# Attention and two MLP layers on one core: x1 in DRAM in the order of the head pairs, read back in pieces of 64 rows

## The chip, the cores and the metric

One core of a Trainium2 chip runs the whole program in one launch. The metric is the device time of that launch in microseconds. Three runs of the kernel before took 959.88, 960.28 and 961.83 us; the median is 960.28 us.

## What is computed

Causal block attention for 4 batches of 8 heads (576 positions, head size 64, blocks of 64 positions), then two MLP layers without normalisation between them. The attention's output x1 has 512 features (8 heads of 64) for each of 2304 tokens.

```python
scores = scale * np.matmul(q, k.transpose(0, 1, 3, 2))   # (4, 8, 576, 576), block-causal mask
attn = softmax(scores)                                    # rows divided by sum + 1e-9
x = np.matmul(attn, v)                                    # (4, 8, 576, 64)
x1 = x.transpose(0, 2, 1, 3).reshape(2304, 512)
h = x1 @ w_in1                                            # 512 -> 2048
g = np.where(h >= 1, h, np.where(h <= -1, 0, (h + 1) ** 2 / 4))
x2 = g @ w_out1                                           # 2048 -> 512
h = x2 @ w_in2
out = (h * np.cos(h)) @ w_out2
```

## The kernel before, in words

The heads are worked on two at a time. A pair fills the 128 partitions with 2 heads of 64 features; 16 pairs cover 4 batches of 8 heads. The list `pairs` names them. The first four pairs (batch 0) are neighbouring heads: (0,1), (2,3), (4,5), (6,7). All later pairs are heads two apart: (0,2), (1,3), (4,6), (5,7), so that one load can bring K or Q of two pairs.

For each pair TensorE makes the scores (L589, the last 64 query rows in L655), ScalarE the exponentials (L605, L668), GpSimd the division (L635), TensorE transposes the probabilities (L692), and then multiplies with V: `pv` (L727) for the main part, `pv_halves` (L738) for what is left of it, `pv_tails` (L784) for the last 64 positions of two pairs. `pv` of pair n reads the tile `rv` (`M.V[n % 2]`, two buffers), which `load_v` fills with three kinds of DMA: L487 (main rows; `pv` waits for these), L491 (the last rows) and L494 (the rows for `pv_halves`). One period of the schedule (the table `PERIOD`) handles two pairs. In it the tails of a pair of pairs are the last readers of both V buffers, so the L487 loads of the next even pair go out only behind them; eight units of TensorE's work later in the table (scores and transposes) stands that pair's `pv`.

The result of a pair is copied out of PSUM to `xs` (128 partitions, 576 columns; three buffers) and stored to `x1d[b]`, a DRAM tile of 512 rows (8 heads of 64 features) and 576 columns: columns 0 to 511 in `pv_halves` (L768), the last 64 columns in `tail_halves` (L806). `x1_rows` (L404) gives the DRAM side of the store. `x1_keys` names what the store writes, for the planner.

Layer 1 works on blocks of two times 256 tokens (one block has a single 256). `x_load` (L820 on) brings a block's x1 back: for each of four groups of 128 features (`kk`) one DMA for each batch that the block touches, of 128 rows (L837). The first block takes x1 straight from `xs`. Then the weights of layer 1 are loaded (L263, L268), put together (ScalarE L280 and L289, VectorE L295), split in two parts, and used by `mm1` (L865) and `mm2` (L906). Weights of layer 2 are combined and written to DRAM between (L341). Layer 2 follows (L1048, L1140).

A planner (`Plan`) sets the order of the program on every engine: each operation has a cost, keys that it reads and writes, and the list of TensorE's own order is kept. All DMAs are issued by SyncE (SP), one after another in the planner's order; an instruction that waits there holds up the ones behind it. In particular SP issues, in this order, in each period: stores of x1, the V loads, then K and Q loads (L527) for later pairs.

```python
pairs = [(b, 2 * p, 2 * p + 1) for b in range(B) for p in range(NP)]
for n in range(NK, N):                       # NK = 4
    b, h, _ = pairs[n]
    pairs[n] = b, h // 4 * 4 + n % 2, h // 4 * 4 + n % 2 + 2
```

Of the kernel before, what the change touches and what calls it, by code (L numbers as in the profile page):

```python
# [9 lines left out]
F32 = mybir.dt.float32  # L10
# [92 lines left out]
def attn_moe_moe_kernel(ctx: ExitStack, tc: tile.TileContext, q, k, v, w_in1, w_out1, w_in2, w_out2, out):  # L103
    nc = tc.nc
    B, H, S, D = q.shape
# [6 lines left out]
    NP = H // 2  # L112
    N = B * NP
# [49 lines left out]
    x1d = [dram.tile([DM, S], F32, name=f"x1d{b}") for b in range(B)]  # L163
# [34 lines left out]
    def do(eng, cost, reads, writes, fn, lock="G", latency=0.0):  # L198
        plan.add(eng, cost, reads, writes, fn, lock, latency)

    def cp(engines, n, out, in_, reads, writes, scale=1.0):
        do(engines, costs(n, engines), reads, writes, lambda e: pin(copy(e, out(), in_(), scale)))

    def diff(engines, n, lo, raw, hi, reads, writes):
        c = {"V": 0.065 + n / 960.0, "G": 0.15 + 0.0022 * n}
        do(engines, {e: c[e] for e in engines}, reads, writes,
           lambda e: pin(rest(lo(), raw(), hi(), nc.gpsimd if e == "G" else nc.vector)), lock="GV")

    def dma(kb, reads, writes, fn):
        do("S", 0.1 + kb / 230.0, reads, writes, lambda e: fn(), latency=2.0)  # L210

    def issue(count, kb, reads, writes, fn, rate=230.0):
        do("S", 0.53 * count, reads, writes, lambda e: fn(), latency=2.0 + max(0.0, kb / rate - 0.53 * count))
# [27 lines left out]
    def x_view(half, kk):  # L241
        arena, off = x_home(half, kk)
        return (M.A1 if half else M.X).view(off, [2, 512], F32R)

    def x_keys(half, kk, part=None):
        arena, off = x_home(half, kk)
        return span(arena, off, 4 * KB) if part is None else span(arena, off + 2 * KB * part, 2 * KB)
# [124 lines left out]
    def split(i):  # L372
        return i > 1

    def pb(at_, b):
        n, i = at_
        if split(i):
            if b not in tiles[n]:
                tiles[n][b] = M.ps[1].tile([128, 512], F32, name=f"t{i}{b}", tag=f"t{i}{b}")
            return tiles[n][b]  # L380
        return whole(at_)[:, b]

    def whole(at_):
        n, i = at_
        if 0 not in tiles[n]:
            tiles[n][0] = M.ps[0].tile([128, 2, 512], F32, name=f"t{i}", tag=f"t{i}")
        return tiles[n][0]

    def bk(at_, b):
        return ("ps", at_[1], b if split(at_[1]) else 0)  # L390

    def bks(at_):
        return [("ps", at_[1], b) for b in range(2 if split(at_[1]) else 1)]

    pairs = [(b, 2 * p, 2 * p + 1) for b in range(B) for p in range(NP)]
    for n in range(NK, N):
        b, h, _ = pairs[n]
        pairs[n] = b, h // 4 * 4 + n % 2, h // 4 * 4 + n % 2 + 2

    def heads(n):  # L400
        _, h0, h1 = pairs[n]
        return slice(h0, h1 + 1, h1 - h0)

    def x1_rows(n, c0, c1):  # L404
        return x1d[pairs[n][0]].rearrange("(h d) s -> h d s", d=D)[heads(n), :, c0:c1]

    def x1_keys(n, part):
        b, h0, h1 = pairs[n]
        return [("x1d", b, h, part) for h in (h0, h1)]


    def tensor(cost, reads, writes, fn):
        do("P", cost + M.switch, reads, writes, lambda e: fn())
# [43 lines left out]
    def pt_view(u):  # L457
        return M.A2.view(PT_HOME[u], [128 * len(PT_BLOCKS[u])])

    def pt_of(i, j):  # L460
        u = i if i == "a" and j != "b" else "b" if i in ("a", "b") else LEFT if (i, j) == (4, 6) else 0 if i < 4 else 2 if i < 6 else 3
        return u, PT_BLOCKS[u].index((i, j))
# [272 lines left out]
    def quarters(at_, jobs):  # L735
        for rows, V, slot, PT, a, b, out_ in jobs:
            for h in range(2):
                pin(nc.tensor.matmul(  # L738
                    out=pb(at_, b)[64 * h:64 * h + 64, out_], lhsT=V[rows, slot, h, :],
                    rhs=PT[rows, a + 64 * (h if rows.start == 0 else 1 - h):][:, 0:64],  # L740
                    start=False, stop=True, skip_group_check=True,
                ))
# [3 lines left out]
    def pv_halves(n):  # L746
        at_ = half_open.pop(n)

        def emit():
            jobs = []  # L750
            for x in range(0, 4, 2):
                u, c = pt_of(2 * x, 2 * x + 2)
                for y, rows, slot in ((x, LOW, x), (x + 1, HIGH, LAST + 1 + x // 2)):
                    o = 128 * (y // 2)
                    jobs.append((rows, M.V[n % 2], slot, pt_view(u), 128 * c, y % 2, slice(o, o + 64)))
            quarters(at_, jobs)

        tensor(0.22, [("V", n % 2)] + [("PT", u, b) for u in (3, 2, 0) for b in range(2)], bks(at_), emit)
        xs = M.xs[n % 3]
        XS = [("xs", n % 3, b) for b in range(2)]  # L760
        to = lambda: xs[:, 0:512].rearrange("p (i b c) -> p b i c", b=2, c=128)
        if split(at_[1]):
            for x in range(2):
                cp("AV", 256, lambda x=x: to()[:, x], lambda x=x: pb(at_, x)[:, 0:256].rearrange("p (i c) -> p i c", c=128),
                   [bk(at_, x)], [XS[x]])
        else:
            cp("AV", 512, to, lambda: whole(at_)[:, :, 0:256].rearrange("p b (i c) -> p b i c", c=128), [bk(at_, 0)], XS)
        issue(1, 256, XS, x1_keys(n, 0), lambda: nc.sync.dma_start(out=x1_rows(n, 0, 512), in_=xs[:, 0:512]))  # L768
        if n < NK:
            t = lambda: x_view(1, n)  # L770
            cp("AG", 512, lambda: t()[:, 0], lambda: xs[:, 0:512], XS, x_keys(1, n, 0))
            diff("V", 512, lambda: t()[:, 1], lambda: xs[:, 0:512], lambda: t()[:, 0],
                 XS + x_keys(1, n, 0), x_keys(1, n, 1))
# [17 lines left out]
    def tail_halves(n):  # L791
        at_ = half_open.pop(("t", n))

        def emit():
            u, c = pt_of("a", "b")
            quarters(at_, [
                (rows, M.V[(n + x) % 2], LAST, pt_view(u), 128 * c, x, slice(0, 64))
                for x, rows in ((0, LOW), (1, HIGH))
            ])

        tensor(0.11, [("V", c) for c in range(2)] + [("PT", u, b) for u in "ab" for b in range(2)], bks(at_), emit)
        for x in range(2):
            m = n + x
            xs = M.xs[m % 3]
            cp("AV", 64, lambda xs=xs: xs[:, 512:S], lambda x=x: pb(at_, x)[:, 0:64], [bk(at_, x)], [("xt", m % 3)])
            issue(1, 32, [("xt", m % 3)], x1_keys(m, 1), lambda xs=xs, m=m: nc.sync.dma_start(  # L806
                out=x1_rows(m, 512, S), in_=xs[:, 512:S]
            ))

# [12 lines left out]
    def x_load(kb):  # L822
        x_half, js = 1 - kb % 2, blocks[kb]
        w = NB * len(js)
        for kk in range(NK):
            t = lambda kk=kk: x_view(x_half, kk)
            pieces, need, done = [], [], 0
            while done < w:
                b, c = divmod(js[0] * NB + done, S)
                n = min(w - done, S - c)  # L830
                need += [("x1d", b, 2 * kk + h, part) for h in range(2) for part in range(2) if (c < 512, c + n > 512)[part]]
                pieces.append((b, c, n, done))
                done += n

            def emit(t=t, kk=kk, pieces=pieces):
                for b, c, n, done in pieces:
                    nc.sync.dma_start(  # L837
                        out=t()[:, 1, done:done + n].bitcast(F32), in_=x1d[b][128 * kk:128 * (kk + 1), c:c + n]
                    )

            dma(w // 2, need, x_keys(x_half, kk, 1), emit)
            cp("AG", w, lambda t=t: t()[:, 0, 0:w], lambda t=t: t()[:, 1, 0:w].bitcast(F32),
               x_keys(x_half, kk, 1), x_keys(x_half, kk, 0))
            diff("V", w, lambda t=t: t()[:, 1, 0:w], lambda t=t: t()[:, 1, 0:w].bitcast(F32),
                 lambda t=t: t()[:, 0, 0:w], x_keys(x_half, kk, 0), x_keys(x_half, kk, 1))
# [452 lines left out]
    def part_one():  # L1298
# [15 lines left out]
        for n in range(2):  # L1314
# [5 lines left out]
        units = {  # L1320
            "tl": tails, "pk": lambda n, t=0: prepare(n, 0, t), "pq": lambda n, t=0: prepare(n, 1, t),
            "PV": pv, "Pt": pv_tails, "PX": pv_halves, "Px": tail_halves,
        }

# [80 lines left out]
        for f, which in wq[EARLY:]:  # L1405
            w_convert(f, which)
        x_load(1)
        for x in range(2, nsteps + 2):
            kb, f = steps[min(x, nsteps - 1)]
# [50 lines left out]
```

## Time and profile before

| what | value |
|---|---|
| median of 3 runs | 960.28 us |
| profiled execution, its own time | 962.15 us |
| span of the profiled execution (first to last instruction) | 960.1 us |
| TensorE busy | 915.9 us (95%) |
| VectorE, ScalarE, GpSimd busy | 664.4, 558.6, 177.5 us |
| TensorE's mean granted clock | 0.973 |
| DMA | 189.90 MB, mean 198 GB/s |
| stores x1d<-xs | 16 of 256 KB, 16 of 32 KB |

The profiled execution took 1.87 us more than the median, and lies 2.05 us above its span. TensorE is busy nearly all the time from about 215 us on; nearly all of its idle time lies in the attention before that. The granted clock is given as a share of the full one; 1.0 is 2.4 GHz and 0.5 is 1.2 GHz. All times in the rows below are microseconds from the start of the span. SPq rows are DMA issues: their duration is that of the issuing instruction, not of the transfer.

### The profile page before, as it was taken

Reading aid. Unit: us, or ns where it says so; the run is one execution under the profiler, and the core shown is the slowest. Engines: PE = TensorE matmul, PEld = TensorE weight load, DVE = VectorE, ACT = ScalarE, POOL = GpSimd, SP = SyncE. Lnnn points to the kernel's source line nnn. Section 1 sums busy time; section 2 is a strip of 40 time slices with the busy share of each in tenths; the row PEclk is TensorE's granted clock in tenths of the full one; section 3 lists DMA queues with packets and bytes.
Section 4 is the critical chain, followed back from the end, with each engine's and each line's share of the span. In section 5 each row is a group of like instructions: output and inputs, shape, how many; then the busy total and the mean of one; then the engine's idle time right before and its main releaser. Section 6 shows DMA issues by size and latency. Waiting matters only on the chain.

```text
span 960.1 us, 17788 instructions
## 1 busy us (share of the span) xinstructions
PE 915.9 (95%) x6738; PEld 818.5 (85%) x6738; DVE 664.4 (69%) x1039; ACT 558.6 (58%) x1030; POOL 177.5 (18%) x300
## 2 busy tenths in 40 slices
PE   8877888989998999999999999999999999999998
PEld 6565667868786888998888888999999999999998
DVE  6668666757875676676644522799977899578883
ACT  6656555668975667666644433668515685156641
POOL 4657454605521221111210000000000000000000
PEclk9889888989998999999999999999999999999999
DMA  7986562547666677575633242787799878887781
GB/s 130 179 166 103 109 108 58 143 149 236 215 220 225 221 241 253 170 264 195 235 123 110 72 147 79 255 257 246 258 305 307 255 248 262 275 269 255 245 260 65
DMA packets 177780, 189.90 MB, mean 198 GB/s; under 512 B 102432, under 2 KB 135712, under 8 KB 177696
## 3 DMA queue, kind: packets, MB, share of 16 engines
q1 hardware_dynamic: 177696, 188.78, 65.3%
q8 instruction: 53, 0.87, 0.4%
q14 instruction: 31, 0.25, 0.1%
HBM read 145.23 MB, written 43.52 MB: 197 GB/s over the span
## 4 chain that ended last, share of the span: by engine, by line
PE 68%; DVE 0%; ACT 0%; issue 0%
PE q L1140 19%; PE q L1048 18%; PE a L906 16%; PE h L865 15%; ACT f L185 0%; ACT o L185 0%; DVE o L1167 0%; DVE o L190 0%; DVE f L295 0%; ACT g L185 0%; DVE f L880 0%; DVE f L181 0%; ACT f L878 0%; ACT f L879 0%
## 5 line engine op out<-in xcount | busy, mean ns | idle before, releaser
L1048 PE MATMUL q<-m 128*128 128x384 f32 x1008 | 175.2, 334 | 0.0
L1048 PEld LDWEIGHTS q<-m 128*128 128x128 f32 x1008 | 174.7, 188 | 0.1
L1140 PE MATMUL q<-m,n 128*128 128x256 f32 x1260 | 153.8, 283 | 0.0
L1140 PEld LDWEIGHTS q<-m,n 128*128 128x128 f32 x1260 | 152.4, 192 | 0.0
L906 PE MATMUL a<-g,m 128*128 128x512 f32 (+1 forms) x540 | 120.5, 372 | 4.5 <-ACT o L185 4.0
L906 PEld LDWEIGHTS a<-g,m 128*128 128x128 f32 x540 | 95.0, 190 | 23.4 <-ACT o L185 4.4
L880 DVE SCALAR_TENSOR_TENSOR f<-f,h 128x512 f32<-128x512 f32 (+1 forms) x80 | 50.5, 631 | 80.7 <-ACT f L879 80.1
L878 ACT ACTIVATE f<-h,half 128x512 f32<-128x512 f32 (+1 forms) x80 | 51.4, 643 | 86.6 <-PE h L865 85.0
L181 DVE TENSOR_TENSOR g<-f,g 128x512 fp32r<-128x512 f32 (+1 forms) x80 | 53.4, 668 | 36.2 <-ACT g L185 31.7
L727 PE MATMUL t<-n,rv 128*64 128x128 f32 (+1 forms) x640 | 43.6, 299 | 27.5 <-DMA rv<-in_v_dram 23.2
L727 PEld LDWEIGHTS t<-n,rv 128*64 128x64 f32 x640 | 40.5, 168 | 33.9 <-issue 25.3
L865 PE MATMUL h<-m 128*128 128x512 f32 (+1 forms) x324 | 67.2, 356 | 0.0
L295 DVE SCALAR_TENSOR_TENSOR f<-f 128x512 uint32<-128x512 uint32 x64 | 49.7, 788 | 23.6 <-ACT f L280 17.4
L865 PEld LDWEIGHTS h<-m 128*128 128x128 f32 x324 | 54.0, 189 | 8.5
L598 DVE TENSOR_REDUCE sm<-t 128x1 f32<-128x512 f32 (+7 forms) x128 | 50.0, 446 | 9.8 <-PE t L589 9.2
L185 ACT ACTIVATE g<-f 128x512 fp32r<-128x512 f32 (+1 forms) x65 | 38.1, 587 | 30.6 <-DVE f L880 30.6
L1017 ACT ACTIVATE f<-f,hpi 128x768 f32<-128x768 f32 x48 | 44.6, 929 | 16.3 <-DVE f L1013 16.3
L635 POOL TENSOR_SCALAR n<-n,sm 128x64 f32<-128x64 f32 (+6 forms) x104 | 49.4, 493 | 22.3 <-ACT P L605 11.1
L865 PE MATMUL h<-x,m 128*128 128x512 f32 x216 | 53.4, 397 | 0.0
L190 DVE COPY n<-t 128x512 f32<-128x512 f32 (+3 forms) x49 | 33.5, 715 | 28.6 <-PE t L692 28.3
L906 PE MATMUL a<-g,n 128*128 128x512 f32 (+1 forms) x240 | 52.8, 368 | 0.0
L289 ACT ACTIVATE f<-f,floor__82 128x512 uint32<-128x512 uint16 x53 | 40.2, 759 | 19.6 <-DMA f<-in_moe_w_in_dram 19.5
(143 smaller groups left out, 1649.3 us busy)
## 6 DMA issues: line engine op xcount, KB each, us to landing
m<-w2i SPq DMA_DIRECT2D x84, 512.0 KB
m<-w2o SPq DMA_DIRECT2D x84, 512.0 KB
f<-in_moe_w_in_dram SPq DMA_DIRECT2D x32, 512.0 KB
f<-in_moe_w_out_dram SPq DMA_DIRECT2D x32, 512.0 KB
w2i<-f SPq DMA_DIRECT2D x8, 1024.0 KB
w2o<-f SPq DMA_DIRECT2D x8, 1024.0 KB
w2i<-o SPq DMA_DIRECT2D x8, 768.0 KB
w2o<-o SPq DMA_DIRECT2D x8, 768.0 KB
```

The lines of the kernel that those rows point to most:

```text
L181: return (eng or nc.vector).tensor_tensor(out=lo, in0=raw, in1=hi.bitcast(F32), op=ALU.subtract)
L295: pin(nc.vector.scalar_tensor_tensor(out=v().bitcast(U32), in0=t.bitcast(U32), scalar=3, in1=w.bitcast(U32), op0=ALU.logical_shift_left, o ...
L598: nc.vector.tensor_reduce(out=stat(0, n, i, i + 1), in_=pb(at_, a)[:, off:off + nk], axis=AX.X, op=ALU.max, negate=True,)))
L635: do("G", 0.25 + 0.00082 * w, sk(2, n, e0, e0 + 1) + [P_(i, n)], [writes], lambda e: pin(nc.gpsimd.tensor_scalar(out=out(), in0=probs(i, m ...
L727: pin(nc.tensor.matmul(out=out_.rearrange("p (e b) -> p e b", b=64) if j < x else out_, lhsT=V[:, j, h, :], rhs=rhs if j < x else rhs[:, 0 ...
L865: pin(nc.tensor.matmul(out=h_of(), lhsT=wt[:, a, kk * 128:(kk + 1) * 128], rhs=x[:, b, 0:w], start=(kk == 0 and i == 0), stop=(kk == NK - ...
L878: nc.scalar.activation(out=g(), in_=h_of(), func=ACTF.Relu, bias=half, scale=0.5)))
L880: do("V", 0.07 + w / 960.0, [H] + E, E, lambda e: pin(nc.vector.scalar_tensor_tensor(out=g(), in0=g(), scalar=1.0, in1=h_of(), op0=ALU.min ...
L906: pin(nc.tensor.matmul(out=o, lhsT=wt[:, a, dm:dm + 128], rhs=b, start=(f == 0 and i == 0 and c == 0), stop=(f == NF - 1 and i == 2), skip ...
L1017: nc.scalar.activation(out=o, in_=a, func=func, **kw)
L1048: pin(nc.tensor.matmul(out=ps[:, e, 0:HT], lhsT=w[:, e, a, 128 * kk:128 * (kk + 1)], rhs=L2.xq[i][:, kk, c], start=(not src and kk == 0 an ...
L1140: pin(nc.tensor.matmul(out=ps[:, m // 2, 256 * (m % 2):256 * (m % 2) + 256], lhsT=t[:, e, a, 128 * m:128 * (m + 1)], rhs=w[:, e, o], start ...
```

## The change

In DRAM the rows of a batch of x1 are put in the order of the pairs: pair n takes rows 128 * (n % 4) to 128 * (n % 4) + 127. A store thus has one range of 128 rows on both sides. Before, the DRAM side of pairs 4 to 15 was a pattern of two heads by 64 rows, 128 rows apart. `x_load` needs neighbouring heads 2kk and 2kk + 1 in one group of 128 partitions. In batch 0 these still lie one behind the other and stay one load. In batches 1 to 3 they lie in two places, so each load becomes two of 64 rows each. In all, 28 loads become 52.

```diff
+    row_of = {(pairs[n][0], pairs[n][1 + x]): 128 * (n % NP) + 64 * x for n in range(N) for x in range(2)}
+
     def x1_rows(n, c0, c1):
-        return x1d[pairs[n][0]].rearrange("(h d) s -> h d s", d=D)[heads(n), :, c0:c1]
-
-    def x1_keys(n, part):
-        b, h0, h1 = pairs[n]
-        return [("x1d", b, h, part) for h in (h0, h1)]
+        return x1d[pairs[n][0]][128 * (n % NP):128 * (n % NP) + 128, c0:c1]
...
-        issue(1, 256, XS, x1_keys(n, 0), lambda: nc.sync.dma_start(out=x1_rows(n, 0, 512), in_=xs[:, 0:512]))
+        issue(1, 256, XS, [("x1d", pairs[n][0], n % NP, 0)], lambda: nc.sync.dma_start(out=x1_rows(n, 0, 512), in_=xs[:, 0:512]))
...
-            issue(1, 32, [("xt", m % 3)], x1_keys(m, 1), lambda xs=xs, m=m: nc.sync.dma_start(
+            issue(1, 32, [("xt", m % 3)], [("x1d", pairs[m][0], m % NP, 1)], lambda xs=xs, m=m: nc.sync.dma_start(
...
-                need += [("x1d", b, 2 * kk + h, part) for h in range(2) for part in range(2) if (c < 512, c + n > 512)[part]]
+                need += [("x1d", b, row_of[b, 2 * kk + h] // 128, a) for h in range(2) for a in range(2) if (c < 512, c + n > 512)[a]]
...
                 for b, c, n, done in pieces:
-                    nc.sync.dma_start(
-                        out=t()[:, 1, done:done + n].bitcast(F32), in_=x1d[b][128 * kk:128 * (kk + 1), c:c + n]
-                    )
+                    rows = [row_of[b, 2 * kk + h] for h in range(2)]
+                    for h, w_ in ([(0, 128)] if rows[1] == rows[0] + 64 else [(0, 64), (1, 64)]):
+                        nc.sync.dma_start(
+                            out=t()[64 * h:64 * h + w_, 1, done:done + n].bitcast(F32),
+                            in_=x1d[b][rows[h]:rows[h] + w_, c:c + n],
+                        )
```

The order of the instructions on TensorE, VectorE, ScalarE and GpSimd is the same as before. On SP two places matter. The first is the middle of a period: the stores of pairs 4 and 5 (`xs_116`, `xs_117`) among the V loads (`rv_109` for even pairs, `rv_110` for odd ones). Before:

```order
L494 DMA rv_109<-in_v_dram 64x2x64 x2
L768 DMA x1d_61<-xs_116 2x64x512
L494 DMA rv_110<-in_v_dram 64x2x64 x2
L768 DMA x1d_61<-xs_117 2x64x512
L487 DMA rv_109<-in_v_dram 128x4x64 x2
L491 DMA rv_109<-in_v_dram 64x2x64
```

The same place with the change (line numbers are two lower here):

```order
L492 DMA rv_109<-in_v_dram 64x2x64 x2
L766 DMA x1d_61<-xs_116 128x512
L492 DMA rv_110<-in_v_dram 64x2x64 x2
L766 DMA x1d_61<-xs_117 128x512
L485 DMA rv_109<-in_v_dram 128x4x64 x2
L489 DMA rv_109<-in_v_dram 64x2x64
```

Nothing moved; the stores' shape went from 2x64x512 to 128x512. The second place on SP is the end of the attention: the last stores of x1, then the weights of layer 1 (`f`) and the loads of the second block's x1 (`x`). Before:

```order
L768 DMA x1d_63<-xs_115 2x64x512
L263 DMA f<-in_moe_w_in_dram 128x4x256
L268 DMA f<-in_moe_w_out_dram 128x1024
L837 DMA x<-x1d_60 128x64
L837 DMA x<-x1d_61 128x448
L837 DMA x<-x1d_60 128x64
L837 DMA x<-x1d_61 128x448
L837 DMA x<-x1d_60 128x64
L263 DMA f<-in_moe_w_in_dram 128x4x256
L268 DMA f<-in_moe_w_out_dram 128x1024
```

The same place with the change:

```order
L766 DMA x1d_63<-xs_115 128x512
L263 DMA f<-in_moe_w_in_dram 128x4x256
L268 DMA f<-in_moe_w_out_dram 128x1024
L837 DMA x<-x1d_60 128x64
L837 DMA x<-x1d_61 64x448 x2
L837 DMA x<-x1d_60 128x64
L837 DMA x<-x1d_61 64x448
L263 DMA f<-in_moe_w_in_dram 128x4x256
L268 DMA f<-in_moe_w_out_dram 128x1024
```

Loads of batch 0 (`x1d_60`) stay whole, loads of batch 1 (`x1d_61`) are in two parts, and the weights' loads stand at a slightly different place among them: five x1 loads ahead of the next weights before, and five now, of which three are half as large, with the rest behind.

## Rows read from the trace of the kernel before

**Rows 1.** Windows: length, busy us per engine (instructions), PEclk, DMA share, GB/s.
```profile
62.79:79.55 16.76, 16.76 (x281) 13.34 (x277) 16.23 (x45) 15.80 (x48) 12.49 (x25) 1.00 0.86 142
79.55:104.72 25.17, 18.32 (x282) 14.77 (x278) 16.59 (x43) 12.88 (x44) 12.54 (x28) 0.86 0.53 102
104.72:127.94 23.22, 18.81 (x281) 15.18 (x277) 16.33 (x43) 12.88 (x44) 12.13 (x26) 0.85 0.69 113
127.94:151.51 23.57, 19.03 (x281) 15.36 (x278) 16.34 (x43) 13.00 (x44) 11.19 (x25) 0.86 0.36 73
151.51:172.07 20.56, 18.05 (x266) 14.20 (x262) 15.55 (x42) 13.24 (x43) 11.23 (x25) 0.92 0.26 65
...
215.00:280.00 65.00, 64.84 (x284) 52.73 (x283) 51.07 (x70) 56.69 (x97) 29.95 (x29) 1.00 0.67 214
...
530.00:960.00 430.00, 425.65 (x2827) 413.51 (x2825) 311.95 (x333) 220.41 (x275) 0.00 (x0) 1.00 0.70 227
```
**Rows 2.** Waits of TensorE, 54 to 215 us: total, times, longest.
```profile
PE t L727 <- DMA rv<-in_v_dram: 23.2, 6, 6.8
```
**Rows 3.** Timeline of TensorE: start, length, what; idle before it and its releaser.
```profile
53.57 4.16 PE L727 MATMUL t<-n,rv 128*64 128x128 f32 x40 [4.86 <-DMA rv<-in_v_dram]
...
72.90 2.00 PE L727 MATMUL t<-n,rv 128*64 128x128 f32 x40
...
87.28 2.17 PE L589 MATMUL t<-K,Q 64*64 64x512 f32 x32
96.30 3.76 PE L727 MATMUL t<-n,rv 128*64 128x128 f32 x40 [6.85 <-DMA rv<-in_v_dram]
```
**Rows 4.** Timeline of SP, 50 to 90 us: DMA issues, start and length of the issue.
```profile
50.23 2.22 SPq L487 DMA_DIRECT2D rv<-in_v_dram  x4
...
62.06 0.90 SPq L768 DMA_DIRECT2D x1d<-xs  x1
...
66.56 0.54 SPq L768 DMA_DIRECT2D x1d<-xs  x1
67.20 1.00 SPq L487 DMA_DIRECT2D rv<-in_v_dram  x2
...
82.42 0.60 SPq L768 DMA_DIRECT2D x1d<-xs  x1
...
84.55 0.54 SPq L768 DMA_DIRECT2D x1d<-xs  x1
85.18 4.69 SPq L487 DMA_DIRECT2D rv<-in_v_dram  x2
```
**Rows 5.** Windows: behind one lone store (issued at 169.34), and after a stall.
```profile
170.50:174.20 3.70, 3.70 (x69) 2.87 (x69) 2.79 (x8) 2.10 (x5) 1.76 (x5) 1.00 0.14 40
96.30:99.60 3.30, 3.30 (x35) 3.21 (x37) 0.00 (x0) 0.00 (x0) 0.00 (x0) 0.50 0.48 89
```
**Rows 6.** Timeline of TensorE: the later stalls of L727.
```profile
119.03 4.04 PE L727 MATMUL t<-n,rv 128*64 128x128 f32 x40 [4.41 <-DMA rv<-in_v_dram]
...
142.38 4.05 PE L727 MATMUL t<-n,rv 128*64 128x128 f32 x40 [4.54 <-DMA rv<-in_v_dram]
...
163.81 3.57 PE L727 MATMUL t<-n,rv 128*64 128x128 f32 x40 [2.41 <-DMA rv<-in_v_dram]
...
197.20 3.68 PE L727 MATMUL t<-n,rv 128*64 128x128 f32 x40 [4.16 <-ACT n L185]
```
**Rows 7.** Timeline of ScalarE ahead of the last stall.
```profile
192.94 0.74 ACT L289 ACTIVATE f<-f,floor__82 128x512 uint32<-128x512 uint16 x1 [4.69 <-DMA f<-in_moe_w_in_dram]
```
**Rows 8.** Timeline of SP, 183 to 216 us.
```profile
183.51 3.59 SPq L263 DMA_DIRECT2D f<-in_moe_w_in_dram  x1
...
204.84 0.49 SPq L768 DMA_DIRECT2D x1d<-xs  x1
...
213.22 2.24 SPq L837 DMA_DIRECT2D x<-x1d  x5
```
**Rows 9.** Timeline of TensorE at the end of layer 1's first block.
```profile
298.78 2.93 PE L906 MATMUL a<-g,m 128*128 128x512 f32 x6 [4.00 <-ACT o L185]
```

## The prediction

> **What bounds the kernel now.** I read the busy time by window first, to see where TensorE is not the limit. From 215 to 280 us it is busy for 64.84 of 65 us, and in layer 2 for 425.65 of 430 us, both at the full clock [rows 1]. There only TensorE's own work counts. The attention is different. The window 62.79:79.55, from one odd pair's `pv` to the next, is one period of 16.76 us with TensorE busy throughout. The next three hold the same work (281 to 282 matmuls) and take 25.17, 23.22 and 23.57 us [rows 1].
>
> The waits say why: 23.2 us in six waits of L727 (`pv`) for the V loads [rows 2]. The timeline of TensorE places them. The first, 4.86 us at 53.57, stands before any store that the change reshapes. The `pv` at 72.90 (pair 4) waits for nothing. Pair 6's waits 6.85 us and starts at 96.30 [rows 3], pairs 8, 10 and 12 wait 4.41, 4.54 and 2.41 us [rows 6]. They begin exactly with the first stores of the two-by-64 shape, those of pairs 4 and 5, at 82.42 and 84.55; the V loads stand right behind them at 85.18 [rows 4].
>
> So how fast does such a store go? Behind the one issued at 169.34 nearly nothing else was under way: the DMA share was 0.14 and the rate 40 GB/s [rows 5]. 0.14 is little more than 2 of 16 engines (0.125). At 40 GB/s or less, 256 KB take at least 262144 / 40000 = 6.6 us, two stores 13.1 us. Counted from 82.42 that is 95.5 us, and TensorE started again at 96.30 [rows 3]. The V loads need all engines, their last parts queue behind the stores on the two engines that are full, and the other fourteen idle (share 0.53 in that period, against 0.86 in the undisturbed one [rows 1]).
>
> By contrast the 128x512 store at 66.56 had V loads behind it at 67.20 [rows 4], and `pv` started at 72.90 without a wait [rows 3].
>
> The Trainium skill, page "DMA: Bandwidth & Descriptors", section "Why a DMA increments its semaphore by 16 and not by 1", states that a DMA runs on the largest number of engines up to 16 that divides the slowest dimension of both its patterns: 2 for 2x64x512, 16 for 128x512 and also for 64 rows. The share of 0.14 agrees; no row here shows it for 64 rows.
>
> **The change part by part.**
>
> *Stores of pairs 4 to 15 become 128x512 (12 of them) and 128x64 (12).* The order on SP stays. I take their speed to be that of the early stores, so the V stalls behind them go. In the three full periods the loss is 25.17 + 23.22 + 23.57 - 3 x 16.76 = 21.68 us [rows 1]. It has two parts: the stalls, and what follows them. The granted clock stood at 0.50 after the stall of pair 6 [rows 5], that is 1.2 in place of 2.4 GHz, and its `pv` took 3.76 us where pair 4's took 2.00 [rows 3]. The fourth period holds other work, so I count pair 12's stall and slow `pv`: 2.41 + 3.57 - 2.00 = 3.98 us [rows 6]. Together **25.7 us**.
>
> *The end of the attention.* `pv` of pair 15 waits 4.16 us for ScalarE [rows 6], which stood 4.69 us on a weights load (L289) [rows 7]. That load was issued at 183.51, took 3.59 us to issue and was there only at 192.94 [rows 8, 7], 9.4 us later, where V loads ahead of any reshaped store were there in 53.57 - 50.23 = 3.34 us [rows 3, 4]. It too lies between stores of x1. With 3.34 to 6 us in its place ScalarE hardly waits. Its stall and the slow `pv` behind it give 4.16 + 3.68 - 2.00 = **5.8 us** [rows 6].
>
> *What is late next: SP.* Without stalls TensorE's period is 16.76 us, but SP's two V issues stand 85.18 - 67.20 = 17.98 us apart [rows 4], in a stretch with eight K and Q loads. Two more periods have those. Pair 4 had 72.90 - 67.20 - 3.34 = 2.36 us to spare. Losing 1.22 us a period, pair 6 has 1.14, pair 8 -0.08, pair 10 -1.30; pair 12 has no K and Q loads ahead. This takes back **1.4 us**. The bounds: nothing, if SP's waits inside that stretch shrink; 10.3 us by the first rival below. I take the low end: a stall of 1.3 us lies below the shortest after which I see a slow `pv` (2.41 us), so I add no clock to it.
>
> *24 more loads of x1* (12 in place of 8 for the second block, 8 for 4, 16 for 8, 16 for 8). One costs SP 2.24 / 5 = 0.45 us [rows 8], in all 10.8 us. It is covered by TensorE's work, which had no gap between 215 and 280 us [rows 1], and by this: the loads of 213.22 went out only 8.4 us behind the last store, that of 204.84, whose `xs` buffer and x1 rows they need [rows 8]. With a faster store they start some 5 us earlier, more than the second block's four extra issues take (1.8 us). Without cover they would cost 10.8 us. I enter them at nothing, since the cover is there in the row; below nothing they can't go, since they only add issues.
>
> The Trainium skill, same page, section "Anatomy of one DMA — SWDGE (gpsimd) path", gives each DMA a fixed cost of about 2.0 us. An estimate by it, one behind another: 24 x 2.0 = 48 us, which would make it 960.3 - 30 + 48 = 978. The row of five issues in 2.24 us [rows 8] speaks for overlap on SP's queue.
>
> *The planner's keys and the weights' loads that change places with x1 loads*: no cost; they move by one or two issues of 0.45 us, under the same cover.
>
> Sum: 25.7 + 5.8 - 1.4 = **30.1 us**. The profiled execution took 962.15 us, so 932.0 for its like; the median of the runs lies 1.87 lower, at 960.28. I predict **930 us**.
>
> **The rivals.**
>
> *SP becomes the bound.* If the queue needs as long in both remaining K and Q periods as between the first stores of two periods, 82.42 - 62.06 = 20.36 us [rows 4], TensorE loses 2 x 3.60 = 7.2, less 0.9 to spare, plus two slow `pv` of 2.0: 10.3 us. Time: 960.3 - 31.5 + 10.3 = 939. Against it: the 17.98 us measured from V load to V load, in the same stretch.
>
> *VectorE becomes the bound.* It is busy 16.23 to 16.59 us a period [rows 1], just under TensorE's 16.76. With waits of its own a period of 18 us would cost some 1.2 us in each of 3.5 periods: 934. Against it: 62.79:79.55 ran at TensorE's pace with VectorE at 16.23.
>
> *The change does not do what it says*: the shape of the store isn't what slows it, or the V loads stay late. Then 959 to 962. Against it: rows 3 to 5 fit in every pair.
>
> *Slower: the split loads are served one after another, each for a whole landing.* Place: the four blocks of layer 1, where the weights' loads stand behind them on SP. Price: 24 x 3.34 = 80 us [rows 3, 4] if all of it is exposed; it decides from about 1.3 us a load, where 24 of them eat the 31.5 us. Time: 960.3 - 30 + 80 = 1010. For it: 0.45 us is only the issue. Against it: in the trace issues go out back to back while earlier ones are still under way [rows 4, 8].
>
> **How the numbers follow.** My forecast (925 to 934) has 0.64, SP as the bound (935 to 941) 0.17, VectorE as the bound (933 to 938) 0.14, no effect 0.03, slower 0.02. The range is 925 to 940. The low end adds the stall of 4.00 us at 298.78 [rows 9], which hangs on ScalarE behind weights loads and may go with them: 31.5 + 4.0 = 35.5. The high end is the first rival. About 0.2%, 1.9 us, is what a measurement can tell from no change; so faster 0.95, same 0.03, slower 0.02.
>
> **What would show it.** Right: L727's waits for `rv` fall from 23.2 us to some 5 to 7, of which 4.86 are the early one; periods of 16.8 to 18 us; DMA share well over 0.14 behind a store; V loads issued in about 1 us per two; x loads a few us behind the last store; TensorE without gaps after that. Wrong: `pv` still waiting behind stores of 128x512, periods over 20 us, or TensorE waiting in `mm1` for x1 or weights in layer 1.

## The result and the profile after

| | before | changed |
|---|---|---|
| median of 4 runs each | 961.06 us (959.88 to 964.22) | 926.93 us (925.35 to 929.23) |
| ratio, 95% interval | | 0.9642 [0.961, 0.9673] |
| profiled execution, its span | 962.15, 960.1 us | 925.35, 923.5 us |
| TensorE busy | 95% | 98% |

The kernel became 3.6% faster: 34.1 us by the medians, 36.8 between the two profiled executions. The prediction had 930 us, range 925 to 940.

The place to look at first is the wait for V [rows 2]. Waits of TensorE in the changed kernel, 40 to 215 us, then 54 to 215 us (total, times, longest):

```profile
PE t L725 <- DMA rv<-in_v_dram: 5.9, 5, 4.4
...
PE t L725 <- DMA rv<-in_v_dram: 1.5, 4, 0.7
```

Before, 23.2 us in six waits; now 5.9, of which 4.4 is the first one, ahead of any reshaped store. After it 1.5 us are left in four. The timeline of TensorE places them (start, length, what; in brackets the wait; these answer to [rows 3, 6, 9]):

```profile
52.75 3.55 PE L725 MATMUL t<-n,rv 128*64 128x128 f32 x40 [4.38 <-DMA rv<-in_v_dram]
...
88.44 2.53 PE L725 MATMUL t<-n,rv 128*64 128x128 f32 x40 [0.31 <-DMA rv<-in_v_dram]
...
120.94 0.66 PE L690 MATMUL t<-ident,n 128*128 128x128 f32 x4 [0.70 <-POOL n L633]
124.42 0.40 PE L725 MATMUL t<-n,rv 128*64 128x128 f32 x2 [0.72 <-DMA rv<-in_v_dram]
...
169.03 2.00 PE L725 MATMUL t<-n,rv 128*64 128x128 f32 x40
...
263.03 1.67 PE L907 MATMUL a<-g,m 128*128 128x512 f32 x6 [0.57 <-ACT o L185]
```

Pair 6, which waited 6.85 us and ran 3.76 at the low clock, waits 0.31 (88.44). Pair 15 (169.03) waits for nothing; it had waited 4.16 us for ScalarE. The stall of 4.00 us at 298.78 has shrunk to 0.57 (263.03).

The same periods as windows (columns as in [rows 1]), from `pv` to `pv` of the odd pairs, then the end of the attention and the place of the stall for `o` in layer 1:

```profile
60.95:78.23 17.28, 17.17 (x281) 13.57 (x278) 16.24 (x45) 15.89 (x48) 12.60 (x26) 1.00 0.84 136
78.23:95.63 17.40, 16.95 (x282) 13.25 (x278) 16.53 (x43) 12.87 (x44) 12.20 (x27) 1.00 0.72 139
95.63:112.88 17.25, 16.94 (x282) 13.25 (x278) 16.34 (x43) 12.86 (x44) 11.66 (x25) 1.00 0.89 144
112.88:131.72 18.84, 17.16 (x281) 13.23 (x277) 16.54 (x43) 12.86 (x44) 11.69 (x25) 1.00 0.78 128
131.72:148.13 16.41, 16.31 (x265) 12.82 (x261) 15.85 (x42) 13.13 (x43) 10.60 (x24) 1.00 0.31 82
148.13:169.03 20.90, 20.64 (x261) 16.80 (x259) 17.17 (x38) 17.65 (x44) 16.03 (x25) 1.00 0.65 187
169.03:173.90 4.87, 4.87 (x104) 4.47 (x104) 4.69 (x9) 3.32 (x9) 0.00 (x0) 1.00 0.57 186
...
262.46:267.28 4.82, 4.25 (x18) 3.49 (x19) 2.74 (x6) 1.03 (x3) 2.56 (x4) 1.00 1.04 373
```

The last three in the kernel before:

```profile
172.07:197.20 25.13, 20.74 (x264) 17.05 (x260) 16.87 (x37) 16.72 (x43) 14.82 (x24) 0.96 0.54 158
197.20:204.91 7.71, 7.29 (x102) 6.57 (x103) 4.27 (x8) 3.82 (x9) 0.00 (x0) 0.69 0.45 159
...
294.78:305.63 10.85, 6.85 (x20) 5.36 (x20) 5.33 (x11) 4.39 (x7) 3.73 (x5) 0.69 0.92 312
```

The granted clock is 1.00 in all windows of the changed kernel; before it was 0.85 to 0.92 in the four periods behind reshaped stores. The DMA share of the first three of these four rose from 0.53, 0.69 and 0.36 to 0.72, 0.89 and 0.78, and the rate from 102, 113 and 73 to 139, 144 and 128 GB/s.

SP's queue, where the stores and the V loads stand (DMA issues; answers to [rows 4, 8]):

```profile
85.32 0.54 SPq L766 DMA_DIRECT2D x1d<-xs  x1
85.96 0.99 SPq L485 DMA_DIRECT2D rv<-in_v_dram  x2
...
173.42 0.38 SPq L766 DMA_DIRECT2D x1d<-xs  x1
...
175.87 2.62 SPq L837 DMA_DIRECT2D x<-x1d  x5
```

Two V issues behind the stores take 0.99 us where they took 4.69: issuing itself was held up. The loads of x1 start 2.45 us behind the last store (175.87 - 173.42), before 8.4.

Behind one lone store, of 145.28, the windows 145.3:147.5 and 147.5:150.3 now show this (before, 0.14 and 40 GB/s [rows 5]):

```profile
145.30:147.50 2.20, 2.10 (x22) 1.67 (x24) 2.20 (x4) 2.09 (x8) 2.20 (x4) 1.00 0.45 149
147.50:150.30 2.80, 2.80 (x61) 2.32 (x55) 2.47 (x8) 1.17 (x3) 2.09 (x7) 1.00 0.02 6
```

After 2.2 us the transfer is over (some of the 149 GB/s belongs to two V loads issued just before it). The two spans differ by 36.6 us; where they come from, stage by stage:

| stage | before | after | gain |
|---|---|---|---|
| start to the first odd `pv` | 62.79 | 60.95 | 1.8 |
| undisturbed period | 16.76 | 17.28 | -0.5 |
| three periods behind reshaped stores | 71.96 | 53.49 | 18.5 |
| fourth period | 20.56 | 16.41 | 4.2 |
| end of attention, to layer 1's first `mm2` | 25.13 + 7.71 | 20.90 + 4.87 | 7.1 |
| first block of layer 1 | 89.87 | 88.56 | 1.3 |
| stall for `o`, with the slow matmuls behind it | 10.85 | 4.82 | 6.0 |
| rest of layer 1, layer 2 | 654.5 | 656.2 | -1.8 |

### The profile page after: what moved, and what is told of

It is laid out like the page before. It is cut to its first block, busy times and chain, and to the rows that moved or that the text cites. A ratio compares the mean times of both kernels' runs of the same rounds, so it can differ in the third digit from the quotient of the medians.

```text
span 923.5 us, 17850 instructions
## 1 busy us (share of the span) xinstructions
PE 902.7 (98%) x6738; PEld 806.9 (87%) x6738; DVE 664.4 (72%) x1039; ACT 558.1 (60%) x1030; POOL 177.5 (19%) x300
## 4 chain that ended last, share of the span: by engine, by line
PE 87%; DMA 4%; ACT 2%; SPq 2%; DVE 2%; issue 1%; POOL 1%; ACTq 0%; DVEq 0%; POOLq 0%
PE q L1141 20%; PE a L907 19%; PE h L866 19%; PE q L1049 19%; PE t L690 3%; PE t L725 3%; PE t L587 2%; DMA rv<-in_v_dram 2%; SPq L837 1%; PE t L782 1%; PE t L653 1%; PE t L736 1%; DMA x2d<-o 1%; POOL n L633 1%; DMA f<-in_moe_w_in_dram 1%
## 5 line engine op out<-in xcount | busy, mean ns | idle before, releaser
L907 PEld LDWEIGHTS a<-g,n 128*128 128x128 f32 x240 | 42.1, 189 | 7.5
L880 ACT ACTIVATE f<-f 128x512 f32<-128x512 f32 (+1 forms) x80 | 46.8, 585 | 1.6
L866 PEld LDWEIGHTS h<-x,m 128*128 128x128 f32 x216 | 40.4, 188 | 8.3
```

The source lines that it names most:

```text
L866: pin(nc.tensor.matmul(out=h_of(), lhsT=wt[:, a, kk * 128:(kk + 1) * 128], rhs=x[:, b, 0:w], start=(kk == 0 and i == 0), stop=(kk == NK - ...
L880: do("A", 0.05 + 0.00084 * w, E, E, lambda e: pin(nc.scalar.activation(out=g(), in_=g(), func=ACTF.Square)))
L907: pin(nc.tensor.matmul(out=o, lhsT=wt[:, a, dm:dm + 128], rhs=b, start=(f == 0 and i == 0 and c == 0), stop=(f == NF - 1 and i == 2), skip ...
```

## The experiments

The medians of before in these comparisons lie between 961.0 and 962.2 us. The theory: a store of 2x64 rows runs on few DMA engines, and V, loaded behind it, is late. Rivals: the order on SP's queue is what matters; other engines bound the periods; the loads in halves matter too.

**The loads alone.** Head order and stores as before, loads of batches 1 to 3 in two.

```diff
+for r, w_ in ([(0, 128)] if b == 0 else [(0, 64), (64, 64)]):
+    nc.sync.dma_start(out=t()[r:r + w_, ...], in_=x1d[b][128 * kk + r:128 * kk + r + w_, c:c + n])
```

> x1 stays in head order and the stores keep their 2x64x512 shape; only the loads of batches 1 to 3 are split in two of 64 rows (52 loads in place of 28). Theory (the stores' two engines hold up what is queued behind them): nothing comes back, 958 to 964 us, the five waits for V and the 4.0 us wait at the end of layer 1's first block stay. Rival (part of the gain comes from the loads' new shape and place on SP): the wait at the end of the first block and its slow stretch go, 952 to 956 us. Rival (each split load costs its landing): 970 us or more.

Measured: 963.22 us (961.46 to 965.72), ratio 1.0021 [1.0009, 1.0032]. Waits of TensorE:

```profile
PE t L727 <- DMA rv<-in_v_dram: 23.9, 6, 6.8
PE t L727 <- ACT n L185: 4.4, 1, 4.4
PE a L908 <- ACT o L185: 3.4, 1, 3.4
```

All stalls stay, the one for `o` at 3.4 us too. The loads alone bring nothing and cost 0.9 to 3.1 us, by the interval of the ratio.

**The stores alone.** Head order kept, each store of pairs 4 to 15 as two DMAs of 64 rows; loads whole.

```diff
+for x in range(2):
+    r = D * pairs[n][1 + x]
+    nc.sync.dma_start(out=x1d[b][r:r + D, c0:c1], in_=M.xs[n % 3][64 * x:64 * x + 64, c0:c1])
```

> x1 stays in head order, the loads stay 28; each store of pairs 4 to 15 is two DMAs, one for each head (64 rows each). Theory: 64 rows spread over all engines too, so the V waits go as with the change; SP has 4 more issues a period (2.2 us), which brings V loads later in the three periods with K and Q loads: 927 to 937 us. Rival (what helps is that a pair's rows lie in one range of DRAM): the V waits stay, 955 to 962 us.

Measured: 934.29 us (933.19 to 936.0), ratio 0.972 [0.9704, 0.9736].

```profile
PE t L734 <- DMA rv<-in_v_dram: 14.4, 6, 7.9
```

7.9 of these 14.4 us fall on the first `pv`, ahead of any changed store; 6.5 are left behind them. Of the stall for `o` 0.57 us are left, as in the changed kernel. So the pattern of the store is the cause, since the order of the rows in DRAM is still the old one here; the new order is one way to get a better pattern. That way is 7 us better. SP issues 24 DMAs more among the V loads here:

```profile
68.66 1.00 SPq L494 DMA_DIRECT2D rv<-in_v_dram  x2
...
88.61 1.14 SPq L494 DMA_DIRECT2D rv<-in_v_dram  x2
...
109.83 1.12 SPq L494 DMA_DIRECT2D rv<-in_v_dram  x2
...
132.26 1.16 SPq L494 DMA_DIRECT2D rv<-in_v_dram  x2
```

The first V issues of the periods stand 19.95, 21.22 and 22.43 us apart, in the changed kernel 18.68, 17.09 and 18.86. This is the prediction's rival "SP becomes the bound", at work in this kernel and not in the changed one.

**V ahead of the stores.** The kernel before, SP issuing each period's stores of x1 behind its V loads.

```diff
-issue(..., lambda: nc.sync.dma_start(out=x1_rows(n, 0, 512), in_=xs[:, 0:512]))
+issue(..., lambda: later(n, lambda: nc.sync.dma_start(out=x1_rows(n, 0, 512), in_=xs[:, 0:512])))
...
+            if n % 2: flush()     # in load_v, behind its last DMA
```

What the cut leaves out: the V loads and these stores are also fixed in that order on SP. Some stores go out here only after `xs` has been filled again, so x1 of a later pair is stored for those pairs: the same bytes, other data.

> The kernel before with its slow stores, but on SP the V loads of the next pairs are issued ahead of the stores of x1 (DMAs of both pinned in that order); nothing else moves on the other engines. Theory (it matters what stands behind a slow store): the V waits of 4.4 to 6.9 us shrink to under 2 us each; the weights' loads at the end of the attention still stand behind stores, so their part stays lost: 936 to 946 us. Rival (a slow store hurts through xs or by itself): V waits vanish but other waits take their place, 955 us or more.

Measured: 960.99 us (957.92 to 963.56), ratio 0.9994 [0.9978, 1.001]. Waits of TensorE:

```profile
PE t L694 <- POOL n L637: 12.2, 5, 6.7
PE a L918 <- DVE xs L190: 9.5, 1, 9.5
PE t L739 <- DMA rv<-in_v_dram: 8.2, 3, 4.2
```

The forecast of 936 to 946 missed. V's waits fell from 23 to 8.2 us, but new ones of about the same size came. They begin on SP: the stores that now stand behind V have the loads of Q behind them. SP, then GpSimd:

```profile
111.71 1.12 SPq L780 DMA_DIRECT2D x1d<-xs  x2
112.94 13.28 SPq L529 DMA_DIRECT2D rq<-in_q_dram  x4
```
```profile
129.86 1.31 POOL L187 TENSOR_SCALAR rq<-rq 128x576 f32<-128x576 f32 x2 [11.36 <-DMA rq<-in_q_dram]
```

Four Q loads take 13.28 us to issue. GpSimd waits 11.36 us for them to scale Q, and only then makes the division that TensorE waits for (6.72 us at 131.58). At the end of the attention it is the weights: ScalarE waits 9.90 us for them (201.10), and the copies of `xs` behind that are the 9.5 us of TensorE. So neither my theory's gain nor the lateness of the `xs` buffers that I had in mind: a slow store holds up whatever is loaded behind it, and the order only chooses what that is.

**V on a queue of its own.** The kernel before, V's loads issued by ScalarE.

```diff
-nc.sync.dma_start(out=t[:, 0:LAST, h, :], in_=src[...])
+nc.scalar.dma_start(out=t[:, 0:LAST, h, :], in_=src[...])
```

> The kernel before (stores of two ranges of 64 rows, head order), with the loads of V issued by ScalarE, on a queue of their own, in place of SP. If V is late because its loads stand behind the slow stores in one queue (order), they now pass them: the waits of TensorE for rv fall from 23.2 to under 8 us and the time to 936 to 946 us, the rest being lost to late xs buffers as in the run with V ahead of the stores. The rival: the two DMA engines that carry a store are busy whatever queue a load comes from, and each V load has a share on them, so V still lands 6 us or more after its issue; then waits of 12 us or more and 950 to 962 us. ScalarE's issues (66 DMAs) may cost it some us of their own in either case.

(The late xs buffers in it are the misreading that the run before has just corrected.)

Measured: 961.87 us (958.95 to 965.47), ratio 1.001 [0.9994, 1.0025]. TensorE no longer waits for `rv`, but for ScalarE. First a store on SP, then ScalarE:

```profile
84.74 0.50 SPq L768 DMA_DIRECT2D x1d<-xs  x1
```
```profile
85.28 0.38 ACTq L487 DMA_DIRECT2D rv<-in_v_dram  x1
...
88.81 0.86 ACTq L487 DMA_DIRECT2D rv<-in_v_dram  x1
93.71 0.60 ACTq L491 DMA_DIRECT2D rv<-in_v_dram  x1
94.41 1.08 ACT L185 ACTIVATE n<-t 128x512 f32<-128x512 f32 x2 [4.07 <-DMA x1d<-xs]
```

TensorE's largest wait:

```profile
PE t L589 <- ACT n L185: 11.3, 4, 4.0
```

By the last semaphore update of each of them in the trace, the loads of 85.28 to 88.81 land 6.9 to 8.4 us after their issue, though no store stands in their queue, and the store lands at 93.69. This is the rival: the engines are taken, whatever queue a load comes from. (The waits for `rv` that it also named did not come; the wait for ScalarE took their place. And the edit moves 80 loads, not 66.)

The single updates show it directly. A V load leaves 16 of them. In the kernel before, the V load of 85.18 has 14 by 89.56 and the last two at 96.15 and 96.16, 0.4 us behind the two of the store of 84.55 (95.73 and 95.74); every V load issued there between 83 and 95 us has such a split of 14 and two. In the changed kernel the V load of 85.96 has all 16 between 87.96 and 88.31. In this run the five V loads of 85.28 to 88.81 have the split again, the last two updates 3.0 to 4.6 us behind the other fourteen, on a queue without stores.

A second effect mixes in. Eight semaphores serve all DMAs of this program in turn, so a DMA can have to wait for an earlier one to land; the load of 93.71 uses that of the store and went out 0.02 us after it landed. Such waits of ScalarE sum to 15.4 us in four. How much of TensorE's loss each effect costs is left open by this run.

**Four ranges of 32 rows.** The changed kernel with two pairs interleaved in DRAM, so that a store is 4x32x512, and loads of 32 rows.

```diff
-return x1d[pairs[n][0]][128 * (n % NP):128 * (n % NP) + 128, c0:c1]
...
+two = x1d[pairs[n][0]][256 * (n % NP // 2):256 * (n % NP // 2) + 256, c0:c1]
+return two.rearrange("(j i r) s -> i j r s", i=2, r=32)[n % 2]
```

> As the change, but a pair's rows lie in four ranges of 32 rows, so its store has the shape 4x32x512; loads of batches 1 to 3 in pieces of 32 rows. Theory (a store's rate goes with the number of its slowest dimension): four engines, share near 0.25 behind a lone store and 70 to 80 GB/s, landing in 4 to 5 us; V waits of 1 to 2.5 us remain in the later periods: 930 to 940 us. Rival (the rate is a matter of two against many, or of the range in DRAM): as the change (925 to 929) or as before (958 to 962).

Measured: 958.11 us (955.31 to 963.88), ratio 0.9979 [0.9961, 0.9998]. The forecast missed by 18 us. Of its theory the share came true: behind the lone store of 140.19 it is 0.23, near 4 of 16 engines. The rate did not, with 60 GB/s (columns as in [rows 1]):

```profile
141.20:145.90 4.70, 4.70 (x93) 3.81 (x95) 4.70 (x11) 3.11 (x14) 0.33 (x1) 1.00 0.23 60
```

V's waits behind such stores are 1.5 to 4.7 us, not 1 to 2.5. Stores and loads were both changed here; the next run changes the loads alone.

**Loads of 32 rows alone.** The changed kernel with its stores of 128 rows.

```diff
-for h, w_ in ([(0, 128)] if rows[1] == rows[0] + 64 else [(0, 64), (1, 64)]):
+for h, w_ in ([(0, 128)] if rows[1] == rows[0] + 64 else [(0.5 * y, 32) for y in range(4)]):
...
```

> The changed kernel with its stores as they are (128 rows as one range), but the loads of blocks 1 to 3 of layer 1 in four pieces of 32 rows in place of two of 64: 48 more loads on SP for x and m together. It sizes what small loads cost once the stores land quickly. By the theory that loads only take SP's issue time (0.42 us each, covered) the time stays at 925 to 930 us and the last pv of attention still starts near 169 us. The rival, raised by the run with four ranges of 32 (958 us, its last pv at 184 us and then 15 us longer than the changed kernel from there to the end): the 32-row loads cost the 15 us; then 938 to 945 us, with attention unchanged and the loss after 197 us, TensorE waiting in layer 1 for g, x or m. If it stays below 930, the loss of that run came with its stores or with what they pushed on SP.

Measured: 937.49 us (936.32 to 939.93), ratio 0.9753 [0.9736, 0.9769]: 10.6 us more than the changed kernel. `pv` of pair 15, first in the run of four ranges, then in this one:

```profile
184.37 2.00 PE L728 MATMUL t<-n,rv 128*64 128x128 f32 x40 [1.60 <-ACT n L185]
```
```profile
170.83 2.00 PE L725 MATMUL t<-n,rv 128*64 128x128 f32 x40
```

The same `pv` starts at 197.20 with stores in two ranges [rows 6], at 184.37 with four, and at 169.03 to 170.83 with one of 128 rows. That is the attention's price of the pattern, in three steps. From that `pv` to its end the run of four ranges takes 15.0 us more than the changed kernel, and this run 12.9, in a profiled execution 2.4 us above its median. So most of the rest of that run's loss comes with the loads; a few us of it are open. Where it arises in this run: SP, GpSimd, TensorE at the second block of layer 1.

```profile
246.69 8.01 SPq L837 DMA_DIRECT2D m<-x1d  x16
254.80 0.38 SPq L341 DMA_DIRECT2D w2i<-f  x1
```
```profile
260.22 0.98 POOL L187 TENSOR_SCALAR f<-f 128x512 fp32r<-128x512 f32 x1 [7.22 <-DMA w2i<-f]
267.72 0.62 POOL L187 TENSOR_SCALAR o<-f 128x512 fp32r<-128x512 f32 x1 [6.52 <-ACT f L185]
```
```profile
269.86 2.93 PE L907 MATMUL a<-g,m 128*128 128x512 f32 x6 [4.98 <-ACT o L185]
```

Sixteen loads hold SP for 8.01 us (eight of 64 rows take 5.17 in the changed kernel). Behind them stands the store of `w2i`, which frees the buffer `f`; GpSimd waits 7.22 us for that, the weights `o` come late, and TensorE waits 4.98 us. A stall of the same kind, of 3.04 us, follows at 357.70. The place is that of [rows 9], and the stall here hangs on SP's lateness. In the kernel before the path differs in one link: GpSimd's wait ahead of `o` (7.81 us at 290.05) ends with VectorE (L335) and not with that store. What both have in common is that the weights run late behind TensorE: the load (L263) that SP issues at 273.93 in the kernel before goes out 69.0 us after the first `mm2` of layer 1, the same load 65.0 us in the changed kernel (238.93) and 67.9 us in this run (243.57).

**Whole loads.** The changed kernel with the 24 extra loads undone.

```diff
-for h, w_ in ([(0, 128)] if rows[1] == rows[0] + 64 else [(0, 64), (1, 64)]):
+for h, w_ in ([(0, 128)]):
...
-in_=x1d[b][rows[h]:rows[h] + w_, c:c + n],
+in_=x1d[b][128 * kk:128 * kk + 128, c:c + n],
```

> The changed kernel with its stores, but x1 of blocks 1 to 3 loaded as 128 rows in one DMA, as before the change. What is read is then the same 128 rows in the order of the pairs, so layer 1 multiplies rows of x1 by the weights of other rows: the same bytes and the same arithmetic, on other data. It is the one part of the change (the 24 extra loads) undone. If the extra loads cost nothing, 925 to 929 us, equal to the changed kernel of the same comparison within 0.2%. The rival, after the 32-row loads (48 more of them cost 10.6 us): each extra load costs about 0.2 us, so 921 to 924 us, most of it where TensorE waits for o in layer 1.

> The changed kernel as it is, in the same comparison as the run with whole loads, since less than half a per cent is to be told apart: 925 to 930 us by either theory.

Measured: 924.51 us (923.52 to 925.31), ratio 0.9619 [0.9597, 0.964], against 927.44 us (925.6 to 930.18), 0.966 [0.9635, 0.9685], of the changed kernel. The medians differ by 2.9 us; the intervals overlap slightly. The traces show 1.8 us of it: from layer 1's second block to the end, 654.5 us with whole loads, as before, and 656.2 to 656.3 in both profiles of the changed kernel. (The whole spans differ by less, 923.0 against 923.5 and 923.8 us, because the first `pv` of the run with whole loads waited 6.89 us for V against 4.38 and 4.44, ahead of anything that its edit touches.) 1.1 us of it arises around here (changed kernel), a group that takes 1.60 us otherwise:

```profile
354.10 2.04 PE L907 MATMUL a<-g,m 128*128 128x256 f32 x12 [0.23 <-ACT g L185]
```

The rest of the 1.8 lies behind TensorE's last matmuls and is not explained.

**Two attempts at a faster kernel.** The changed kernel with the early weights' loads begun one pair later (`FROM_PAIR` 2 in place of 1), and with V's loads issued by ScalarE.

> The changed kernel with the early loads of layer 1's weights begun at pair 2 of attention in place of pair 1, so that the first loads of V have fewer DMAs ahead of them. If the wait that is left at the first pv (4.38 us at 52.75, with one window of low clock at 52.1) comes from those weights, it goes, worth 4 to 7 us: 919 to 923 us. The rival: that wait is the V load's own distance behind the stores on SP and stays, 925 to 930 us; and where the weights are then late at the end of attention, ScalarE waits there for f as in the kernel before, 2 to 7 us slower, 928 to 934 us.

> The changed kernel with the loads of V issued by ScalarE in place of SP. What is left there of waits for rv is 5.9 us, 4.4 of it at the first pv, and SP is some 13 us late at the end of attention by the spacing of the V loads. If that wait is SP's lateness, V lands earlier and the time is 919 to 924 us. The rival: the first V loads are late for another reason, and ScalarE pays for 66 issues (at most 0.4 us each, about 26 us of its time, some of it ahead of the softmax that TensorE waits for): 926 to 940 us.

Measured: 929.42 us (926.87 to 930.52), ratio 0.9662 [0.9643, 0.9681], and 935.55 us (932.29 to 936.6), ratio 0.9729 [0.9705, 0.9752]. Neither beats the changed kernel. In the first, the wait at the first `pv` is still there:

```profile
54.68 3.76 PE L725 MATMUL t<-n,rv 128*64 128x128 f32 x40 [6.40 <-DMA rv<-in_v_dram]
```

So beginning the weights a pair later does not take it away; 6.40 us lies within the 4.4 to 6.9 us that this wait takes in runs which change nothing ahead of it. In the second no wait for `rv` is left at all, and ScalarE pays for it early, with its copy to `xs`:

```profile
PE t L690 <- ACT xs L185: 7.4, 1, 7.4
```

## Why the prediction was right

*V's stalls and the clock behind them (25.7 us, less 1.4 for SP).* This was right: 18.5 us in three periods and 4.2 in the fourth, 22.6 against 24.3. The mechanism was the one named: the stores of pairs 4 and 5 have their last semaphore updates at 90.36 and 95.74 in the kernel before, where the sum of their transfers had 95.5, and the V loads' last two updates come right behind. What is missing lies in the three periods, which stand 0.6, 0.5 and 2.1 us above the undisturbed 16.76 where the sum had 0, 0.1 and 1.3. Of these 3.2 us 2.4 are idle time, 1.68 in the period 112.88:131.72 alone: waits for V, and 0.70 for GpSimd, which itself stood 4.06 us on Q loads (115.80). Both are late on SP: its first V issues of the full periods stand at 67.28, 85.96, 103.05 and 121.91, so 18.68, 17.09 and 18.86 us apart where I took 17.98. "What is late next: SP" was the right name, and 1.4 us about half of what it takes back. (That term counts pair 8's 0.08 twice, since pair 10's 1.30 has it; 1.3 would be right. And "0.9 to spare" in the rival has no source, the term above it gives 1.14; the rival stays at 939.)

*End of the attention (5.8 us).* This was right, and gave 7.1. Behind the one `pv` that I counted 1.2 us more were lost: 0.7 in matmuls at the low clock (0.69 in 197.20:204.91), 0.4 in a wait for the copies of `xs`.

*The stall for `o` at 298.78 [rows 9].* This is the term that was mis-sized: entered at nothing and put in the low end of the range at 4.0 us. It gave 6.0, since the low clock behind it (0.69 in 294.78:305.63) went as well; in the second profile of the changed kernel 1.42 us of the stall are left. Stores alone (0.57 us left) and loads alone (3.4 us left) show that it came from the slow stores. That it did so by way of weights that run late behind TensorE fits the issue times on SP and the run with loads of 32 rows, but no run isolates it. The sum counted 30.1 us, the two profiles differ by 36.8 and the medians by 34.1; this stall is most of the rest.

*The 24 loads (nothing).* This was nearly right, and wrong in its reason. "The cover is there in the row" held for TensorE's work up to 280 us, but not to 298.78 and 354, where TensorE stands close behind GpSimd and ScalarE, and they behind SP. They cost 1.8 us by the traces and 2 to 3 by the times, about 0.1 us each. 48 more cost 10.6, 0.22 each: about twice the price per load. That the slack is used up is my reading; the loads there are also half as large, and no run separates the two.

*The rivals.* SP as the bound (939) is seen in its beginnings only; with two DMAs for a store it came true. VectorE as the bound fell: 16.2 to 16.5 us a period in periods of 17.3 to 18.8, with no stall of TensorE on it. "The change does not do what it says" and "each split load costs a landing" fell with the first two experiments. Of the signs of being right one failed: a period of 18.84 us, above the 16.8 to 18 that were named.

*The rules of the Trainium skill, page "DMA: Bandwidth & Descriptors".* A store of 2x64 rows leaves 3 updates of its semaphore in the trace, one of 4x32 leaves 5, and one of 128 rows 16. This agrees with the section "Why a DMA increments its semaphore by 16 and not by 1": 2, 4 and 16 engines (with one update more in the first two). Stores of 64 rows (in the run with the stores alone) and loads of 64 and of 32 rows also leave 16; the prediction had no row for that. The 2.0 us of the section "Anatomy of one DMA — SWDGE (gpsimd) path" are given there for DMAs on GpSimd's path; these loads go out on SP's queue, and the prediction's estimate took them one behind another. The runs do not bear it out: 24 more loads cost 1.8 to 3 us and not 48.

*One inaccuracy ahead of the prediction:* SP does not issue the stores of x1 first and the V loads behind them. The parts of the V loads stand among the stores, as the order shown there and [rows 4] have it, and the run with V ahead of the stores had to fix SP's order by hand.

## What to carry to other kernels

Before a store is laid out in DRAM, look at what its pattern does to the transfer: if the DMA share behind a lone transfer is near a small multiple of 1/16 (0.14 with two ranges here, 0.23 with four), a single range of 128 rows, even at the price of twice as many loads later, can be worth far more than the transfer itself, since whatever is loaded behind it waits, in its own queue or another, and so does a DMA whose turn it is on the same semaphore. Price extra DMAs by the slack of whoever stands behind them on the same queue, and not by TensorE's cover alone. A stall late in a program can be the echo of an earlier one: follow it back along the queues before entering it as a constant.

## What was not expected of the hardware

- Twice the engines did not halve the landing. Stores of 256 KB with little else under way land 7.7 to 7.8 us after issue in two ranges of 64 rows (kernel before), 5.9 to 6.0 in four of 32, and 2.2 to 2.3 in one of 128 (changed kernel) (from their last semaphore updates).
- Issuing is held up as well: two V loads behind such stores take 4.69 us to issue [rows 4], four Q loads 13.28, and two V loads 0.99 behind stores of 128 rows (single issues of up to 2.4 us stand in the changed kernel too).
- A queue of its own does not protect a load from a slow store on another queue: 6.9 to 8.4 us to land, where V's median in the changed kernel is 2.7 us, by the view of its tile:

```profile
DMA to landing us min/median/max: 2.0/2.7/5.0
```
